# Windowed attention into a two-layer network: even tokens stored first, adjacent heads paired, DMA transposes written straight to their place

## The chip, the cores and the metric

One core of a Trainium2 chip. TensorE (PE) multiplies matrices into PSUM, VectorE (DVE), ScalarE (ACT) and GpSimd (POOL) work on SBUF (DVE and ACT also on PSUM), SyncE (SP) issues most DMAs, and POOL issues those that cast the weights. The metric is the device time of one execution in microseconds (us). Times within the execution come from one profiled run; a line number such as L265 is a line of the kernel before.

## The reference

```python
# q, k, v: 8 batches, 8 heads, 576 tokens, 64 features each
scores = (q @ k.T) / sqrt(64)
scores = where(abs(i - j) <= 32, scores, -1e9)     # a window of 65 tokens
attn = exp(scores - max); attn = attn / sum(attn)
x = (attn @ v), heads side by side                 # 4608 tokens x 512
h = x @ w_in                                       # 512 -> 2048
g = maximum(0.01 * h, h)
out = g @ w_out                                    # 2048 -> 512, float32
```

## The kernel before

**Attention, in tiles.** Heads are taken in pairs, head p with head p + 4, four pairs per batch. A tile is one pair with one half of the tokens (288 of 576): i counts 64 tiles, and `where(i)` gives batch, half and pair. The keys of a pair lie in `kbd` (and the values in `vbd`) in nine blocks of 64 tokens, each block a 128x128 matrix with one head in either diagonal corner and zeros elsewhere, so one matmul serves both heads. Each buffer exists twice, for even and odd batches. A query token sees two neighbouring key blocks, or one near an edge; the table WIN lists per half five (block, first query, count) entries whose columns sum to 544.

For each tile, `score` (L249) runs five matmuls into the PSUM tile `ps`, ACT takes the exponential of 544 columns into `e`, and POOL multiplies by a 0/1 mask (L265) into one of six places of `prob`. The odd blocks' columns lie behind the even blocks' columns, and one of the two parts is 32 columns shorter. `join` (L269) adds the two parts on DVE, reading into zero pads; with it `sums` (L279) needs one matmul with a matrix of ones, without it two (256 and 288 columns). Tiles from JOINED = 12 on are joined. DVE takes the reciprocal (L296). `product` (L299) runs five matmuls with `vbd`, and `scaled` (L320) multiplies by the reciprocal into `xT`, a ring of four halves. PSUM holds one `ps`, one `s` and one `x`.

**Getting queries and keys there.** `load_qk` (L66) puts six consecutive tokens of a head into each of 96 partitions (1536 bytes in a run). `cast_qk` (L177) makes bf16 copies `qb`, `kb`. Transposed, these have the tokens in the order c, i (token 6i + c). For batches 0 to 2 PE transposes them (L214) into PSUM; from batch BY_DMA = 3 on a DMA does, into `tdma` tiles. Either way ACT then copies them to token order (L222 for qT, L228 for kT), and `place_keys` (L235) has DVE copy kT into `kbd`, two copies for a pair.

**The network.** A group g is 288 tokens. `h_tile` (L346) runs four matmuls of 288 columns (L336) for each of 16 feature blocks, and `h_out` (L341) evacuates through ACT with the leaky ReLU into `gT`. `o_tile` (L364) runs 16 matmuls of 512 columns (L373) for 128 tokens; ACT evacuates (L378) and SP stores. Both share four PSUM buffers.

**Order.** Each engine executes its instructions in the order in which the program issues them. The start is written out by hand (L473 to L581): batch 0, the first group and its weight loads (POOL, L465 and L471), then the second half, batch 1 and group 1. From there a plan lists h and o work with a cost each, `due` spreads the four tiles of a group over the time before its start, and `spend` (L608) issues a `step` when one is due. A step issues the join of tile i + 1, transposes, the score of i + 2, then sums, product and scaling of tile i, then key placement, casts, DMA transposes and loads for later batches. The table PLAN and the conditions at L423 to L456 and L630 say in which step of a batch each of those stands.

Of the kernel before, what the change touches and what calls it, by code (L numbers as in the profile page):

```python
# [16 lines left out]
def kernel(  # L17
# [11 lines left out]

    nc = tc.nc  # L30
# [12 lines left out]
    NCOL = 544  # L43
# [10 lines left out]
    tdma = ctx.enter_context(tc.tile_pool(name="tdma", bufs=1))  # L54
# [9 lines left out]

    def load_qk(b, p, behind=None):


        for into, src, name in ((qf, q, "qf"), (kf, k, "kf")):
            t = fload.tile([96, 2, RUN * D], FP32, name=f"{name}{p}")
            if behind is not None:  # L70
                behind.memset(t[0:1, 0, 0:1], 0.0)
                behind = None
            nc.sync.dma_start(  # L73
                out=t, in_=src[b, p:H:NPAIR].rearrange("a (p c) d -> p a (c d)", c=RUN),
            )
            into[b, p] = t

    def load_v(b, p):

        t = fload.tile([128, NB, D], FP32, name=f"vf{p}")  # L80
        for a in range(2):
            nc.sync.dma_start(
                out=t[64 * a:64 * a + 64],
                in_=v[b, NPAIR * a + p].rearrange("(c p) d -> p c d", p=64),
            )
# [30 lines left out]
    def clear(t, p):  # L116
# [12 lines left out]

    PAD = 32  # L130
    SPLIT = [HALF - PAD, HALF]
    WIN = [
        [(1, 32, 128), (3, 160, 128), (0, 0, 96), (2, 96, 128), (4, 224, 64)],
        [(4, 288, 64), (6, 352, 128), (8, 480, 96), (5, 288, 128), (7, 416, 128)],
    ]

    win = const.tile([128, 3, 128], BF16)
    nc.gpsimd.memset(win, 1.0)
    for lo in (0, 64):
# [3 lines left out]
            base=0, channel_multiplier=-1, pattern=[[0, 3], [1, 128]],  # L143
# [3 lines left out]
            base=2 * W, channel_multiplier=1, pattern=[[0, 3], [-1, 128]],  # L147
        )
    nc.gpsimd.memset(vbd[0][:, 3], 0.0)
    win_f = win.rearrange("p n c -> p (n c)")  # L150
    mask = [const.tile([128, NCOL], BF16, name=f"mask{i}") for i in range(2)]

    def make_masks():
        for hf in range(2):
            lo = (0, 2 * W)[hf]
            nc.gpsimd.tensor_copy(
                out=mask[hf][:, 0:SPLIT[hf]], in_=win_f[:, lo:lo + SPLIT[hf]],
            )
            lo = (W, 0)[hf]
            nc.gpsimd.tensor_copy(  # L160
                out=mask[hf][:, SPLIT[hf]:NCOL], in_=win_f[:, lo:lo + NCOL - SPLIT[hf]],
            )
    NPROB = 6
    prob = const.tile([128, NPROB, NCOL + 2 * PAD], BF16)
    nc.vector.memset(prob[:, :, 0:PAD], 0.0)
    nc.vector.memset(prob[:, :, PAD + NCOL:], 0.0)

# [9 lines left out]
    def cast_qk(b, p, q_eng=None):  # L177
        for eng, src, dst in ((q_eng or nc.gpsimd, qf, qb), (nc.gpsimd, kf, kb)):
            tok = src[b, p].rearrange("p a (c d) -> p c a d", d=D)
            if eng is nc.scalar:  # L180
                eng.activation(out=dst[:, p], in_=tok, func=AF.Copy)
            else:
                eng.tensor_copy(out=dst[:, p], in_=tok)  # L183
# [9 lines left out]

    BY_DMA = 3
    qkT, asked = {}, {}

    def transpose_dma(b, p):
        for which, src in (("q", qb), ("k", kb)):
            t = tdma.tile([128, RUN, 96], BF16, name=f"{which}T{p}")
            nc.sync.dma_start_transpose(out=t, in_=src[:, p].rearrange("p c a d -> p (c a d)"))  # L200
            qkT[b, p, which] = t
        asked[b, p] = state["done"]

    def transposes(b):

        qT[b] = attn.tile([128, NPAIR, S], BF16, name="qT")
        for p in range(NPAIR):
            for which, src in (("q", qb), ("k", kb)):
                if b >= BY_DMA:
                    tp = qkT.pop((b, p, which))  # L210
                else:
                    tp = mmps.tile([128, RUN, 96], BF16, name="tp", tag="mm")
                for c in range(RUN if b < BY_DMA else 0):
# [6 lines left out]
                tok = tp.rearrange("p c i -> p i c")  # L220
                if which == "q":
                    nc.scalar.activation(  # L222
                        out=qT[b][:, p].rearrange("p (i c) -> p i c", c=RUN), in_=tok, func=AF.Copy,
                    )
                else:
                    kT = kt.tile([128, S], BF16, name="kT")
                    kT_v = kT.rearrange("p (i c) -> p i c", c=RUN)
                    nc.scalar.activation(out=kT_v, in_=tok, func=AF.Copy)  # L228
# [3 lines left out]
    unplaced = []  # L232

    def place_keys():

        while unplaced:
            b, p, kT = unplaced.pop(0)
            for a in range(2):
                r = slice(64 * a, 64 * a + 64)
                nc.vector.tensor_copy(  # L240
                    out=kbd[b % 2][r, p, :, r],
                    in_=kT[r].rearrange("p (n j) -> p n j", j=64),
# [7 lines left out]
    def score(i):  # L250
        b, hf, p = where(i)
        ps = scps.tile([128, 1024], FP32, name="ps")
        lo = c0 = 512 - SPLIT[hf]
        for blk, q0, n in WIN[hf]:
            nc.tensor.matmul(  # L255
                ps[:, c0:c0 + n], kbd[b % 2][:, p, blk],
                qT[b][:, p, q0:q0 + n], start=True, stop=True,
            )
            c0 += n
        e = attn.tile([128, NCOL], BF16, name="e")  # L260
        nc.scalar.activation(  # L261
            out=e, in_=ps[:, lo:lo + NCOL], func=AF.Exp, scale=scale,
        )
        pr = prob[:, i % NPROB, PAD:PAD + NCOL]
        nc.gpsimd.tensor_mul(pr, e, mask[hf])  # L265
        probs[i] = [pr, None, None]
        state["ps"] = ps

    def join(i):  # L269


        hf = where(i)[1]
        lo = PAD * hf
        t = prob[:, i % NPROB]
        both = joined.tile([128, HALF], BF16, name="both")
        nc.vector.tensor_add(both, t[:, lo:lo + HALF], t[:, lo + HALF:lo + 2 * HALF])  # L276
        probs[i][1] = both

    def sums(i):  # L279
# [6 lines left out]
        else:  # L286
            nc.tensor.matmul(
                s, ones_bd, pr[:, (NCOL - HALF) * (1 - hf):(NCOL - HALF) * (1 - hf) + HALF],
                start=True, stop=False, skip_group_check=True,
            )  # L290
            nc.tensor.matmul(
# [378 lines left out]
```

The softmax here doesn't subtract the row's maximum and nothing guards it: scores larger than these inputs give would overflow.

## Time and profile before

| | us |
|---|---|
| median of 6 runs | 323.42 |
| lowest and highest | 322.3, 323.62 |
| the profiled execution | 323.6 |
| its span | 321.9 |
| PE, ACT, DVE, POOL busy | 304.5, 223.9, 213.9, 182.4 |
| weight loads into PE | 205.5 |
| 40 ACT copies to token order, batches 3 to 7 (L222, L228) | 47.2 |
| 24 ACT evacuations of PE transposes, batches 0 to 2 | 15.7 |
| 144 PE transposes, modelled busy time | 11.6 |
| 64 DVE copies into kbd (L240) | 28.5 |
| 56 POOL casts of q and k (L183) | 48.4 |

The span runs from the first to the last instruction of the profile. Busy times of PE are modelled and overlap one another, so the time that a matmul holds PE is better read from the start of the next one. The clock that was granted to PE was 1.00 in every stretch. In the profile's lines, "idle before <- X" is the time that an engine stood still ahead of such an instruction and what ended it.

### The profile page before, as it was taken

Reading aid. Unit: us, or ns where it says so; the run is one execution under the profiler, and the core shown is the slowest. Engines: PE = TensorE matmul, PEld = TensorE weight load, DVE = VectorE, ACT = ScalarE, POOL = GpSimd, SP = SyncE. Lnnn points to the kernel's source line nnn. Section 1 sums busy time; section 2 is a strip of 40 time slices with the busy share of each in tenths; the row PEclk is TensorE's granted clock in tenths of the full one; section 3 lists DMA queues with packets and bytes.
Section 4 is the critical chain, followed back from the end, with each engine's and each line's share of the span. In section 5 each row is a group of like instructions: output and inputs, shape, how many; then the busy total and the mean of one; then the engine's idle time right before and its main releaser. Section 6 shows DMA issues by size and latency. Waiting matters only on the chain.

```text
span 321.9 us, 6584 instructions
## 1 busy us (share of the span) xinstructions
PE 304.5 (95%) x2497; PEld 205.5 (64%) x2497; DVE 213.9 (66%) x259; ACT 223.9 (70%) x432; POOL 182.4 (57%) x215
## 2 busy tenths in 40 slices
PE   1669999999999999999999999999999999999995
PEld 1457775586765857676664857676665857676653
DVE  5678975976757779677838778677747666565100
ACT  7577594296658897888887887888885837464531
POOL 8799967667946876169623896269612653230000
PEclk9999999999999999999999999999999999999999
DMA  8999999999997999829994399929611000000101
GB/s 178 212 173 225 268 242 217 273 223 227 211 185 197 230 232 234 161 86 173 184 224 124 91 205 221 188 71 138 166 39 65 36 34 35 32 36 0 67 33 66
DMA packets 85168, 48.28 MB, mean 150 GB/s; under 512 B 64016, under 2 KB 80656, under 8 KB 85136
## 3 DMA queue, kind: packets, MB, share of 16 engines
q1 hardware_dynamic: 80848, 43.66, 64.1%
q0 software_dynamic: 4288, 4.20, 8.0%
q8 instruction: 19, 0.31, 0.4%
q14 instruction: 13, 0.11, 0.1%
HBM read 36.70 MB, written 9.44 MB: 143 GB/s over the span
## 4 chain that ended last, share of the span: by engine, by line
PE 84%; DVE 6%; DMA 3%; ACT 2%; POOL 1%; SPq 1%; issue 1%; DVEq 0%; ACTq 0%
PE mm L336 36%; PE mm L373 36%; PE x L307 4%; PE ps L255 4%; DVE r L296 4%; DMA kf<-in_k_dram 3%; PE s L285 2%; DVE xT L322 1%; SPq L73 1%; PE tp L214 1%; DVE qb L183 1%; ACT kT L228 1%; POOL w_in_bf L465 1%; ACT qT L222 1%; DVE kbd L240 1%
## 5 line engine op out<-in xcount | busy, mean ns | idle before, releaser
L296 DVE RECIPROCAL r<-s 128x288 f32<-128x288 f32 x64 | 125.1, 1955 | 56.8 <-PE s L285 53.5
L336 PE MATMUL mm<-xT,w_in_bf 128*128 128x288 bf16 x1024 | 134.0, 286 | 0.3 <-DVE xT L322 0.2
L265 POOL TENSOR_TENSOR prob<-e,mask 128x544 bf16<-128x544 bf16 x64 | 77.8, 1215 | 99.4 <-ACT e L261 81.0
L373 PE MATMUL mm<-w_out_bf,gT 128*128 128x512 bf16 (+2 forms) x592 | 130.4, 373 | 0.0
L342 ACT ACTIVATE gT<-mm 128x288 bf16<-128x288 f32 x256 | 103.6, 414 | 24.2 <-PE mm L336 9.5
L336 PEld LDWEIGHTS <-w_in_bf 128*128 128x128 bf16 x1024 | 97.9, 98 | 24.6 <-issue 0.6
L373 PEld LDWEIGHTS <-gT 128*128 128x128 bf16 x592 | 56.0, 98 | 59.3
L378 ACT ACTIVATE o_sb<-mm 128x512 f32<-128x512 f32 (+2 forms) x37 | 21.7, 586 | 53.2 <-PE mm L373 53.2
L261 ACT ACTIVATE e<-ps 128x544 bf16<-128x544 f32 x64 | 39.8, 621 | 10.5 <-PE ps L255 8.4
L191 POOL CAST vbd<-vf 64x576 bf16<-64x576 f32 x58 | 38.5, 664 | 3.2 <-DMA vf<-in_v_dram 1.4
L240 DVE COPY kbd<-kT 64x576 bf16<-64x576 bf16 x64 | 28.5, 445 | 15.6 <-ACT kT L228 14.9
L322 DVE TENSOR_TENSOR xT<-x,r 128x288 bf16<-128x288 f32 x64 | 29.3, 458 | 8.5 <-PE x L307 1.8
L183 POOL CAST kb<-kf 96x768 bf16<-96x768 f32 x32 | 28.6, 897 | 3.8 <-DMA kf<-in_k_dram 3.7
L255 PEld LDWEIGHTS <-kbd 128*128 128x128 bf16 x320 | 21.5, 99 | 10.2 <-DVE kbd L240 1.4
L255 PE MATMUL ps<-qT,kbd 128*128 128x128 bf16 (+2 forms) x320 | 26.3, 214 | 1.8 <-DVE kbd L240 1.2
L307 PE MATMUL x<-prob,vbd 128*128 128x128 bf16 (+2 forms) x320 | 26.0, 213 | 1.1 <-DVE xT L322 1.0
L307 PEld LDWEIGHTS <-vbd 128*128 128x128 bf16 x320 | 21.4, 99 | 3.9 <-DVE xT L322 1.0
L222 ACT ACTIVATE qT<-qT 128x576 bf16<-128x576 bf16 x20 | 23.6, 1182 | 0.0
L228 ACT ACTIVATE kT<-kT 128x576 bf16<-128x576 bf16 x20 | 23.6, 1182 | 0.0
L276 DVE TENSOR_TENSOR both<-prob 128x288 bf16<-128x288 bf16 x52 | 22.8, 438 | 0.6
L183 POOL CAST qb<-qf 96x768 bf16<-96x768 f32 x24 | 19.8, 824 | 0.0
L285 PE MATMUL s<-both,ones_bd 128*128 128x288 bf16 x52 | 14.9, 286 | 0.0
(45 smaller groups left out, 102.3 us busy)
## 6 DMA issues: line engine op xcount, KB each, us to landing
qf<-in_q_dram SPq DMA_DIRECT2D x32, 288.0 KB, 4.5
kf<-in_k_dram SPq DMA_DIRECT2D x32, 288.0 KB, 4.6
vf<-in_v_dram SPq DMA_DIRECT2D x64, 144.0 KB, 5.0
out_dram<-o_sb SPq DMA_DIRECT2D x35, 256.0 KB, 2.8
w_in_bf<-in_moe_w_in_dram POOLq DMA_DIRECT2D x8, 256.0 KB, 7.3
w_out_bf<-in_moe_w_out_dram POOLq DMA_DIRECT2D x4, 512.0 KB, 15.5
qT<-qb SPq DMA_TRANSPOSE x20, 4.0
kT<-kb SPq DMA_TRANSPOSE x20, 3.3
```

Source lines behind the costliest of these rows:

```text
L183: eng.tensor_copy(out=dst[:, p], in_=tok)
L191: nc.gpsimd.tensor_copy(out=vbd[b % 2][r, p, :, r], in_=vf[b, p][r])
L240: nc.vector.tensor_copy(out=kbd[b % 2][r, p, :, r], in_=kT[r].rearrange("p (n j) -> p n j", j=64),)
L255: nc.tensor.matmul(ps[:, c0:c0 + n], kbd[b % 2][:, p, blk], qT[b][:, p, q0:q0 + n], start=True, stop=True,)
L261: nc.scalar.activation(out=e, in_=ps[:, lo:lo + NCOL], func=AF.Exp, scale=scale,)
L265: nc.gpsimd.tensor_mul(pr, e, mask[hf])
L296: nc.vector.reciprocal(r, s)
L307: nc.tensor.matmul(x[:, a:a + n], vbd[b % 2][:, p, blk, :], pr[:, c0:c0 + n], start=(n_ == 0), stop=(n_ == len(WIN[hf]) - 1), skip_group_c ...
L322: nc.vector.tensor_mul(place(i), x, r)
L336: nc.tensor.matmul(h[:, 0:HALF], w_in_bf[:, c, ts(f, 128)], xT[:, c, ds(g * HALF % RING, HALF)], start=(c == 0), stop=(c == DMC - 1),)
L342: nc.scalar.activation(out=gT[:, f, ds(g * HALF % RING, HALF)], in_=h[:, 0:HALF], func=AF.Prelu, alpha=0.01,)
L373: nc.tensor.matmul(o[:, lo:hi], gT[:, f, ds(128 * j % RING, 128)], w_out_bf[:, f, lo:hi], start=(f == 0), stop=(f == FFC - 1),)
```

## The change

- A pair is heads 2p and 2p + 1. The feature order of x is then the reference's, and a w_in load is one DMA over 128 partitions instead of two over 64.
- From `qT` to the first layer, the 288 tokens of a half are kept with the even tokens first, then the odd ones. Scores, masks, prob, sums, x and xT are in this order; `h_out` puts the tokens back in their order when it reads PSUM. Keys and values keep token order in kbd and vbd: `place_keys` now writes every second element.
- From batch 2 on (BY_DMA = 2), `load_qk` puts tokens in pairs (runs of 512 bytes), each cast is made in two parts, and the transposing DMA writes `qT` and `kT` itself. ACT's copies to token order disappear for these batches. A key pair is placed from two steps after its DMA was asked for.
- Both parts of a tile are 288 columns, the shorter with 32 columns that the mask sets to zero; the exponential and the mask product cover 576. `ps` is one tile that is kept for the whole run.
- JOINED is 9. Casts, transposes and loads of a batch have fixed steps (qk_due, v_due) in place of PLAN. In the start, batch 1's loads stand behind another weight load, and the second half of batch 0 stands at f = 7, 11, 14.

```diff
-    NCOL = 544
+    EVEN = HALF // 2
...
+            heads = src[b, 2 * p:2 * p + 2]
+            if b < BY_DMA:
+                nc.sync.dma_start(out=t, in_=heads.rearrange("a (p c) d -> p a (c d)", c=RUN))
+            else:
+                nc.sync.dma_start(
+                    out=t.rearrange("p a (g e) -> p a g e", g=3),
+                    in_=heads.rearrange("a (g p c) d -> p a g (c d)", g=3, c=2),
+                )
...
     WIN = [
-        [(1, 32, 128), (3, 160, 128), (0, 0, 96), (2, 96, 128), (4, 224, 64)],
-        [(4, 288, 64), (6, 352, 128), (8, 480, 96), (5, 288, 128), (7, 416, 128)],
+        [((0, 0, 48), (2, 48, 64), (4, 112, 32)), ((1, 16, 64), (3, 80, 64))],
+        [((4, 0, 32), (6, 32, 64), (8, 96, 48)), ((5, 0, 64), (7, 64, 64))],
     ]
...
+                by_c = src[b, p].rearrange("p a (g c d) -> c p g a d", g=3, c=2)
+                parts = [(dst[:, p, 3 * c:3 * c + 3], by_c[c]) for c in range(2)]
...
-    BY_DMA = 3
     def transpose_dma(b, p):
-        for which, src in (("q", qb), ("k", kb)):
-            t = tdma.tile([128, RUN, 96], BF16, name=f"{which}T{p}")
-            nc.sync.dma_start_transpose(out=t, in_=src[:, p].rearrange("p c a d -> p (c a d)"))
-            qkT[b, p, which] = t
-        asked[b, p] = state["done"]
+        if b not in qT:
+            qT[b] = attn.tile([128, NPAIR, S], BF16, name="qT")
+        kT = kt.tile([128, S], BF16, name="kT")
+        for t, src in ((qT[b][:, p], qb), (kT, kb)):
+            nc.sync.dma_start_transpose(
+                out=t.rearrange("p (c i) -> p c i", c=RUN),
+                in_=src[:, p].rearrange("p c a d -> p (c a d)"),
+            )
+        landing.append((state["done"], b, p, kT))
...
     def place_keys():
+        while landing and landing[0][0] + 2 <= state["done"]:
+            unplaced.append(landing.pop(0)[1:])
...
-                    out=kbd[b % 2][r, p, :, r],
-                    in_=kT[r].rearrange("p (n j) -> p n j", j=64),
+                    out=kbd[b % 2][r, p, :, r].rearrange("p n (m c) -> p n c m", c=2),
+                    in_=kT[r].rearrange("p (c n m) -> p n c m", c=2, n=NB),
...
+        by_c = qT[b][:, p].rearrange("p (c i) -> p c i", c=2)
+        for n_, blocks in enumerate(WIN[hf]):
+            for blk, i0, n in blocks:
+                nc.tensor.matmul(
+                    ps_v[:, n_, :, i0:i0 + n], kbd[b % 2][:, p, blk],
+                    by_c[:, :, hf * EVEN + i0:hf * EVEN + i0 + n], start=True, stop=True,
+                )
+        e = attn.tile([128, 2 * HALF], BF16, name="e")
+        nc.scalar.activation(out=e, in_=ps[:, P0:P0 + 2 * HALF], func=AF.Exp, scale=scale)
...
     def h_out(g, f, h):
         nc.scalar.activation(
-            out=gT[:, f, ds(g * HALF % RING, HALF)], in_=h[:, 0:HALF], func=AF.Prelu, alpha=0.01,
+            out=gT[:, f, ds(g * HALF % RING, HALF)].rearrange("p (i c) -> p i c", c=2),
+            in_=h[:, 0:HALF].rearrange("p (c i) -> p i c", c=2), func=AF.Prelu, alpha=0.01,
         )
...
-    JOINED = 12
+    JOINED = 9
...
+    for b in range(2, B):
+        for p in range(NPAIR):
+            qk_due.setdefault(8 * (b - 1) + p + (3 if b == 2 else 2), []).append((b, p))
+            v_due.setdefault(8 * (b - 1) + p + 6, []).append((b, p))
...
         place_keys()
+        for b, p in qk_due.get(i, ()):
+            cast_qk(b, p)
+            transpose_dma(b, p)
+            if b + 1 < B:
+                load_qk(b + 1, p)
+        for b, p in v_due.get(i, ()):
+            cast_v(b, p)
+            if b + 1 < B:
+                load_v(b + 1, p)
...
     def load_w_in(f0, f1):
-        for a in range(2):
-            nc.gpsimd.dma_start(
-                out=w_in_bf[64 * a:64 * a + 64, :, f0:f1], in_=w_in_r[a, :, :, f0:f1],
-            )
+        nc.gpsimd.dma_start(out=w_in_bf[:, :, f0:f1], in_=w_in_r[:, :, f0:f1])
...
+    next(h0)
+    next(h0)
+    score(5)
+    load_w_out(1)
     for p in range(NPAIR):
         load_qk(1, p, nc.gpsimd if p == 0 else None)
...
-        if f in (7, 10, 13):
+        if f in (7, 11, 14):
             second_half()
```

## The prediction

> **What bounds the kernel now.** I read the page's totals and slices first, then the table by stretches of 10 us, the groups by shape, the chain of work that ended last, and the timelines of single engines around each gap.
>
> ```profile
> PE 304.5 (95%) x2497; PEld 205.5 (64%) x2497; DVE 213.9 (66%) x259; ACT 223.9 (70%) x432; POOL 182.4 (57%) x215
> ...
> PE   1669999999999999999999999999999999999995
> ...
> PE 84%; DVE 6%; DMA 3%; ACT 2%; POOL 1%; SPq 1%; issue 1%; DVEq 0%; ACTq 0%
> ```
>
> TensorE (PE) is full in every slice from about 25 us to the end. The 70% of ScalarE (ACT) is an average beside it, so an ACT instruction that disappears is worth nothing unless PE waited for it. By stretch:
>
> ```profile
> 40.00:50.00 10.00, 9.57 (x107) 6.95 (x105) 7.72 (x9) 7.98 (x19) 6.12 (x7) 1.00 1.19 235
> 110.00:120.00 10.00, 10.00 (x76) 6.21 (x74) 6.61 (x11) 9.53 (x16) 8.34 (x11) 1.00 1.25 216
> 120.00:130.00 10.00, 9.52 (x84) 6.99 (x82) 8.90 (x11) 8.06 (x18) 5.95 (x7) 1.00 1.23 236
> ```
>
> The columns are the length, then busy time and count of PE, weight loads, DVE, ACT and POOL, then the clock (1.00 throughout), DMA share and GB/s. After 60 us, 120 to 130 is the only whole stretch before the last in which PE is under 10.00; ACT is at 9.53 just before it. Its cause is in PE's timeline:
>
> ```profile
> 121.49 0.28 PE L285 MATMUL s<-both,ones_bd 128*128 128x288 bf16 x1
> 122.05 0.41 PE L307 MATMUL x<-prob,vbd 128*128 128x128 bf16 x5 [0.28 <-DVE xT L322]
> ...
> 126.45 0.41 PE L307 MATMUL x<-prob,vbd 128*128 128x128 bf16 x5 [0.19 <-DVE xT L322]
> ```
>
> In starts, not modelled ends: undisturbed, the s matmul begins 0.24 us after the score and x 0.12 us after s. Here s begins 0.11 us late (121.14 to 121.49) and the two x 0.44 and 0.36 us late: 0.91 us lost. DVE's two copies into kbd stood behind ACT's reordering copies. So two parts can pay: fewer PE instructions, and a shorter start.
>
> **Rows that price the change.**
>
> ```profile
> L342 ACT ACTIVATE gT<-mm 128x288 bf16<-128x288 f32 x256 | 103.6, 414 | 24.2 <-PE mm L336 9.5
> ...
> L322 DVE TENSOR_TENSOR xT<-x,r 128x288 bf16<-128x288 f32 x64 | 29.3, 458 | 8.5 <-PE x L307 1.8 <-PE mm L336 0.5
> ...
> L240 DVE COPY kbd<-kT 64x576 bf16<-64x576 bf16 x64 | 28.5, 445 | 15.6 <-ACT kT L228 14.9
> ...
> L222 ACT ACTIVATE qT<-qT 128x576 bf16<-128x576 bf16 x20 | 23.6, 1182 | 0.0
> ...
> L222 ACT ACTIVATE qT<-tp 128x576 bf16<-128x576 bf16 x12 | 7.8, 648 | 4.8 <-PE tp L214 4.8
> ```
>
> The two L222 rows do the same reordering. Read with a stride from SBUF it takes 1182 ns; from PSUM, 648.
>
> ```profile
> 15.35 0.82 POOL kb L183
> 16.17 2.58 POOL w_in_bf L465 x4
> 18.75 1.25 POOL prob L265
> ...
> 41.91 0.44 DVE kbd L240
> 42.37 0.45 DVE kbd L240
> 42.85 3.00 DVE qb L183
> 45.89 0.68 PE tp L214 x12
> ...
> 68.37 0.26 PE tp L214 x6
> ```
>
> The chain: POOL's weight-load issues hold up a product early on; two kbd copies and a cast hold up transposes at 45.89; a group of six transposes takes 0.26 us of PE.
>
> **1. Transposes of batch 2 leave PE.** 8 groups x 0.26 = **-2.1 us**, all on the bound engine. The DMAs that replace them run on SP's queue. Joining from tile 9 instead of 12 removes three second sum matmuls; the non-joined L291 holds PE 0.11 us (start 56.01 to the next at 56.12), so -0.3. Nine others grow from 256 to 288 columns, by L287's 0.12 against 0.11: +0.1. **Sum -2.3.** Scores and products keep five matmuls and 544 columns per tile, now in two runs each. No matmul here has two runs; contiguous rows are nearest, so no cost.
>
> **2. ACT copies go.** 40 copies x 1.182 = 47.3 us, and 8 evacuations x about 0.65 = 5.2 us, leave ACT. PE waited for these only in the 0.91 us above: **-0.9**. Next late there would be DVE's queue (part 4).
>
> **3. h_out reads its PSUM bank at a stride.** 256 instructions, now even token, odd token, even token, 576 bytes apart. From 512 elements in 597 ns (L378) and 288 in 414, ACT takes 179 ns plus 0.817 per element; that gives 650 for the 576 strided elements of the PSUM row, which took 648. So a stride in PSUM costs nothing there, and I take 414. The other end, from the SBUF row: (1182-179)/576 = 1.74 ns per element, hence 680 ns. PE is the cover: four L336 matmuls take 0.49 us (0.98 per 8 in the chain). At 680 it is gone. [...]
> The exp over 576 instead of 544 columns costs 26 ns more, 64 times, beside PE.
>
> **4. kbd copies write every second element.** 64 DVE copies. The lower end is today's 445. L322 takes 458 ns for 288 elements, and DVE's memsets of 64 and 2304 words (112 and 1978 ns) give 0.83 ns for each further element: 458 + 288 x 0.83 = 698. The upper end is the strided ACT row, 1182. I take 0.70 us, the nearest: same engine. [...]
> In the steady state a step has 4.05 us of dense PE work plus 0.6 of attention, some 4.5 us. DVE needs join 0.44 + reciprocal 1.96 + xT 0.46 + two copies 1.4 = 4.3 in half of the steps, 2.9 in the others: it fits, barely. The copies stand behind xT and two steps ahead of the score that reads them (one in batch 2). No charge.
>
> **5. DMA and POOL in batches 2 to 7.** POOL's product grows from 1215 to about 1286 ns; each q or k cast becomes two. From 664 ns at 576 elements and 824 at 768, 384 take about 0.5. A step's POOL work is 1.3 + 4 x 0.5 = 3.3 us of 4.5, and the product stands first. After the step's product SP issues two transposes (1.2 to 1.3 us each) and lands the last 3.3 us later: about 2.5 + 2.0 + 2.6 + 3.3 = 10.4 us from the step's start. DVE reaches the copy after 9 + 2.9 = 11.9 us: 1.5 us to spare. Loads of q and k have three times the packets, at 512 bytes: between today's 4.5 us and twice the 5.0 of a v load with as many packets; 4.5 is nearer, same bytes. They are asked seven steps ahead (three in batch 2). SP's queue carries the same stores behind them. No charge, bounds 0 to +1.5.
>
> **6. The start.** w_in loads go from two issues each to one of w_out's shape (0.8 us): the 2.58 us before the product of tile 2 becomes 1.6, -1.0. But two kbd copies for pair 3, ending at 19.3, end 0.5 later, at 19.8, and hold the next reciprocal (20.47, or 19.5 without them): what stays is some **-0.6**. At 41.91 two copies cost 0.5 more and the cast behind them starts later; PE already waits 0.4 for it: **+0.5**. Loads of batch 1 start about 1 us later, behind one w_out load, and three joins of 0.3 to 0.5 enter DVE's queue ahead of reciprocals of tiles 8 to 10, where PE waited 0.15 us already: between 0 and +1, taken **+0.3**. Spreading the second half over f = 7, 11, 14 moves waits of 0.24 and 0.34 for the reciprocals without shortening DVE's line: 0.
>
> **Sum.** -2.3 - 0.9 - 0.6 + 0.5 + 0.3 = -3.0 us. The profiled execution took 323.6 us: a span of 321.9 and 1.7 around it. That gives **320.6**. The median of the runs is 323.42, 0.2 under the profiled one. The case's own range is 319.6 to 322.3.
>
> **The rivals.**
> *The start takes it back* (0.15): if the casts wait for batch 1's loads (POOL waited 1.8 us for kf at 42.61, DMA share 1.19), the second pairs and step 8 slip another 1.5 to 2 us: about 322.6.
> *The start gives more* (0.09): kbd copies at 445 ns keep the full -1.0 and drop +0.5: 319.7, with fewer waits 319.2.
> *DVE becomes the bound* (0.08), on the slower side: it decides where a copy exceeds (4.5 - 2.86) / 2 = 0.82 us. At 1182 ns a placing step needs 5.2 us, 0.7 too long; four in a row make 2.8, of which some 1.2 is spare, so 1.6 for each of six batches, and 1.5 more at the start: 332. For it: DVE is already at 8.90 in the stretch above. Against it: DVE's own rows are all under the limit.
> *h_out slow* (0.05): at 680 ns, 16 tiles and two exps need 12.2 us where PE needs 9.0; the four PSUM buffers hide about 2: +1.2 in 15 groups, 339.
> *The DMA path does not serve in time* (0.03): landing 3 us later than reckoned, DVE stops 1.5 us at a copy; a third of it reaching PE in 24 steps gives +12: 333. For it: DMA share above 1 up to 130 us; against it: loads asked seven steps ahead.
>
> **How the numbers follow.** The forecast has 0.60. The range, 318.8 to 323.6, holds the first three cases and leaves out 0.16. About 0.3%, 1 us, is what a measurement of this kernel can tell from no change. Faster: 0.58 of the forecast, 0.09, and 0.03 of the start's rival, 0.70. Same: 0.02 and 0.12, 0.14. Slower: 0.16.
>
> **What would show it.** PE matmuls 2446, no transposes after 51 us, PE 10.00 in each stretch from 60 to 310; no qT<-qT or kT<-kT rows and ACT near 173 us busy; gT<-mm at 414 ns; kbd copies near 700 ns; w_in issues near 0.8. Wrong if gT<-mm is above 0.5 us, if PE waits for kbd or r after 60 us, if POOL waits for qf or kf, or if the first transposes of batch 1's pair 2 come after 46.5 us.

## The result, and the profile after

The changed kernel takes **324.06 us** (median of 19 runs, 323.16 to 325.21). The kernel before took 323.01 in 43 runs beside them (322.3 to 323.67). The ratio is 1.0034, with an interval of 1.0025 to 1.0043: about 1 us slower, where 3 us faster was forecast. The profiled execution of the changed kernel took 323.77 us, a span of 322.1 and 1.7 around it, against 323.6 and 321.9 before. So the two profiled executions differ by 0.2 us, the medians by 1.05. The traces are read for where time was won and lost; that difference of 0.85 is spread between runs, and one execution of each can't place it. One run of experiment 7, of 326.05 us, counts as one in the chip's slower state and is left out of its median there.

The page of the kernel after, its totals, PE's slices and its chain of waits:

```profile
PE 303.3 (94%) x2446; PEld 203.4 (63%) x2446; DVE 226.8 (70%) x263; ACT 179.0 (56%) x384; POOL 198.1 (62%) x259
...
PE   2679899999989999999999999999999999999996
...
PE 81%; DVE 10%; POOL 3%; issue 2%; ACT 1%; DMA 1%; DVEq 0%; POOLq 0%; ACTq 0%
```

PE has the 2446 matmuls that were forecast, 51 fewer. ACT fell from 223.9 to 179.0 us. DVE rose by 13 us, and its share of the chain from 6% to 10%: more of the chain runs through DVE now. The table by stretches of the kernel after, with the columns of the same table before:

```profile
40.00:50.00 10.00, 8.94 (x97) 6.65 (x95) 7.10 (x8) 8.24 (x20) 5.25 (x7) 1.00 1.21 249
...
80.00:90.00 10.00, 9.29 (x70) 6.01 (x68) 5.94 (x8) 5.90 (x14) 5.58 (x7) 1.00 1.17 179
90.00:100.00 10.00, 9.17 (x68) 5.67 (x69) 6.58 (x9) 3.95 (x8) 4.78 (x7) 1.00 1.01 213
120.00:130.00 10.00, 10.00 (x86) 7.29 (x85) 8.52 (x11) 6.27 (x15) 7.21 (x9) 1.00 0.83 182
```

The stall at 121 to 126 us is gone (10.00 where 9.52 stood). In its place 40 to 50 lost more (8.94 after 9.57), and a new hole stands on both sides of 90 us. The groups by shape of the kernel after that the forecast had priced:

```profile
L350 ACT ACTIVATE gT<-mm 128x288 bf16<-128x288 f32 x256 | 103.8, 413 | 23.7 <-PE mm L343 5.2
...
L255 DVE COPY kbd<-kT 64x576 bf16<-64x576 bf16 x64 | 47.8, 747 | 8.6 <-ACT kT L238 4.5 <-DMA kT<-kb 3.5
...
L438 POOL DMA_DIRECT2D w_in_bf<-in_moe_w_in_dram x4 | 3.3, 820 | 0.0
```

All three stand near their forecast: 413 ns (414), 747 ns (700), 820 ns (0.8 us). No single mean is far off, and yet the sum is.

**Where the time went.** PE runs the same attention tiles in the same order in every version, so the start of a tile's first score matmul in PE's timeline is a common mark. In us from the span's start; the rows other than the first two are told below:

```
score of tile           4      9     14     18     19     28     63
before              21.44  47.28  64.18  84.37  89.38 130.62 287.36
after               22.00  48.63  65.81  84.13  90.83 131.15 287.89
after - before      +0.56  +1.35  +1.63  -0.24  +1.45  +0.53  +0.53
unit step           21.13  46.83  64.61  82.80  89.16 129.48 286.22
token order         21.01  46.45  64.30  82.75  89.76 130.08 286.82
step 2 in before    21.54  48.82  65.73  86.63  91.86 133.35 290.09
mended              20.79  46.25  63.28  81.41  86.42 126.73 283.47
mended - before     -0.65  -1.03  -0.90  -2.96  -2.96 -3.89  -3.89
```

The kernel after loses 1.6 us up to tile 14, wins 1.9 where the transposes of batch 2 left PE, loses 1.7 in front of tile 19, and wins 0.9 at 121 to 126 us. So both promised gains are there, and two losses of 1.6 and 1.7 us stand against them.

**The first loss: copies that wait beside POOL.** Rows of the kbd copies, with the shortest, median and longest duration in ns. The kernel before:

```profile
L240 DVE COPY kbd<-kT x64: 399/448/451, 7.7 to 244.9; 64x576 bf16<-64x576 bf16 x64
```

The kernel after:

```profile
L255 DVE COPY kbd<-kT x64: 495/678/2954, 7.8 to 266.4; 64x576 bf16<-64x576 bf16 x64
```

Before, 64 copies are all alike. After, one of them takes six times another. What sets it is in the timelines of DVE and then of POOL, kernel after (start, length, then the instruction; in brackets the idle time before it):

```profile
42.62 1.05 DVE L255 COPY kbd<-kT 64x576 bf16<-64x576 bf16 x2 [1.97 <-ACT kT L238]
43.69 0.56 DVE L196 CAST qb<-qf 96x768 bf16<-96x768 f32 x1
45.09 3.48 DVE L255 COPY kbd<-kT 64x576 bf16<-64x576 bf16 x2 [0.84 <-ACT kT L238]
```

```profile
45.25 0.97 POOL L196 CAST kb<-kf 96x768 bf16<-96x768 f32 x1 [2.89 <-DMA kf<-in_k_dram]
46.16 2.04 POOL L549 MEMSET vbd<- 128x1152 bf16 x2
```

With POOL idle the pair of copies takes 1.05 us. Beside POOL's cast and memsets the next pair takes 3.48, and the score of tile 9, which reads these keys, starts at 48.63 after PE had waited 1.06. The pair ends at 48.57, 0.37 us after the second memset (48.20). The whole kernel shows the same: 55 of its 64 copies begin while a cast, memset or product of POOL is running, and each of the 55 ends 0.36 to 0.40 us after the end of such an instruction. So the copy stands until POOL's instruction is done, here through three of them in a row, and then needs its 0.37 us. In the kernel before, the end of a copy has no such tie to POOL (0.09 to 0.43 us after an end, or none within the copy). A like spread was to be read in the kernel before, in DVE's cast of the queries, which the forecast passed over:

```profile
L183 DVE CAST qb<-qf x7: 714/1318/2986, 4.8 to 46.7; 96x768 bf16<-96x768 f32 x7
```

Seven equal casts, from 714 to 2986 ns. The 3.00 us cast at 42.85, shown in the prediction, ran beside POOL's cast and memsets of the kernel before and ended 0.41 us after them:

```profile
42.61 0.82 POOL L183 CAST kb<-kf 96x768 bf16<-96x768 f32 x1 [1.80 <-DMA kf<-in_k_dram]
43.38 2.05 POOL L578 MEMSET vbd<- 128x1152 bf16 x2
```

The kbd copies around it kept 0.45.

**The second loss: batch 2's keys come late.** SP's queue issues the transposes and the loads. Its timeline in the kernel after:

```profile
78.59 1.46 SPq L211 DMA_TRANSPOSE qT<-qb  x1
80.16 1.20 SPq L211 DMA_TRANSPOSE kT<-kb  x1
81.42 0.57 SPq L81 DMA_DIRECT2D qf<-in_q_dram  x1
82.04 0.50 SPq L81 DMA_DIRECT2D kf<-in_k_dram  x1
82.58 1.30 SPq L91 DMA_DIRECT2D vf<-in_v_dram  x2
83.98 1.83 SPq L211 DMA_TRANSPOSE qT<-qb  x1
85.92 1.93 SPq L211 DMA_TRANSPOSE kT<-kb  x1
```

The queue has hardly a gap. POOL's cast of pair 3's keys ended at 79.10 (the line "77.70 1.40 POOL L196 CAST kb<-kf" of its timeline), but their transpose was issued from 85.92 to 87.85. Then DVE, and then PE, in the kernel after:

```profile
86.77 0.46 DVE L329 TENSOR_TENSOR xT<-x,r 128x288 bf16<-128x288 f32 x1
89.74 1.03 DVE L255 COPY kbd<-kT 64x576 bf16<-64x576 bf16 x2 [2.52 <-DMA kT<-kb]
```

```profile
84.74 4.57 PE L343 MATMUL mm<-xT,w_in_bf 128*128 128x288 bf16 x36
90.83 0.41 PE L270 MATMUL ps<-qT,kbd 128*128 128x96 bf16 x5 [1.51 <-DVE kbd L255]
```

DVE stood 2.52 us for the transfer, whose issue had begun 3.8 us earlier, and PE 1.51 us for DVE.

### The profile page after: what moved, and what is told of

Read it like the earlier page. It is cut to its first block, busy times and chain, and to the rows that moved or that the text cites. A ratio compares the mean times of both kernels' runs of the same rounds, so it can differ in the third digit from the quotient of the medians.

```text
span 322.1 us, 6482 instructions
## 1 busy us (share of the span) xinstructions
PE 303.3 (94%) x2446; PEld 203.4 (63%) x2446; DVE 226.8 (70%) x263; ACT 179.0 (56%) x384; POOL 198.1 (62%) x259
## 4 chain that ended last, share of the span: by engine, by line
PE 81%; DVE 10%; POOL 3%; issue 2%; ACT 1%; DMA 1%; DVEq 0%; POOLq 0%; ACTq 0%
PE mm L343 35%; PE mm L382 35%; DVE r L304 5%; PE x L315 4%; PE ps L270 4%; DVE kbd L255 4%; PE s L296 2%; DVE xT L329 1%; DMA kT<-kb 1%; POOL kb L196 1%; POOL prob L277 0%; ACT e L275 0%; PE tp L224 0%; ACT vbd L202 0%; POOL win L147 0%
## 5 line engine op out<-in xcount | busy, mean ns | idle before, releaser
L277 POOL TENSOR_TENSOR prob<-e,mask 128x576 bf16<-128x576 bf16 x64 | 81.7, 1276 | 84.8 <-issue 42.4
L255 DVE COPY kbd<-kT 64x576 bf16<-64x576 bf16 x64 | 47.8, 747 | 8.6 <-ACT kT L238 4.5
L275 ACT ACTIVATE e<-ps 128x576 bf16<-128x576 f32 x64 | 41.4, 647 | 17.7 <-PE ps L270 16.1
L204 POOL CAST vbd<-vf 64x576 bf16<-64x576 f32 x58 | 40.3, 695 | 1.7
L196 POOL CAST kb<-kf 96x384 bf16<-96x384 f32 (+1 forms) x56 | 36.0, 663 | 4.8 <-DMA kf<-in_k_dram 4.7
L270 PEld LDWEIGHTS <-kbd 128*128 128x128 bf16 x320 | 20.5, 99 | 15.4 <-DVE kbd L255 6.6
L196 POOL CAST qb<-qf 96x384 bf16<-96x384 f32 x48 | 24.4, 535 | 0.0
L287 DVE TENSOR_TENSOR both<-prob 128x288 bf16<-128x288 bf16 x55 | 20.8, 378 | 0.8
L224 PE MATMUL tp<-ident,qb 96*128 96x96 bf16 x48 | 4.4, 242 | 5.8 <-DVE qb L196 5.7
L224 PEld LDWEIGHTS <-qb 96*128 96x128 bf16 x48 | 3.5, 117 | 6.8 <-DVE qb L196 6.4
```

What stands on the lines that cost most here:

```text
L196: eng.tensor_copy(out=to, in_=tok)
L204: nc.gpsimd.tensor_copy(out=vbd[b % 2][r, p, :, r], in_=vf[b, p][r])
L255: nc.vector.tensor_copy(out=kbd[b % 2][r, p, :, r].rearrange("p n (m c) -> p n c m", c=2), in_=kT[r].rearrange("p (c n m) -> p n c m", c=2 ...
L270: nc.tensor.matmul(ps_v[:, n_, :, i0:i0 + n], kbd[b % 2][:, p, blk], by_c[:, :, hf * EVEN + i0:hf * EVEN + i0 + n], start=True, stop=True,)
L275: nc.scalar.activation(out=e, in_=ps[:, P0:P0 + 2 * HALF], func=AF.Exp, scale=scale)
L277: nc.gpsimd.tensor_mul(pr.rearrange("p n c i -> p (n c i)"), e, mask[hf].rearrange("p n c i -> p (n c i)"),)
```

## The experiments

The theory after the first reading was that the form of the kbd copy (every second element) made it wait for POOL, and that the lateness of batch 2 was a matter of SP's queue or of full DMA engines. Rivals were that the 512-byte packets of the new loads were the cause, and that the earlier joins or the order of the start's loads were. Where the quoted expectations use letters for theories, the text names them in words. Times are medians; a ratio is against the kernel before, run beside it, which had medians of 322.96 to 323.1, and need not be the quotient of two medians. A wait of PE is the bracket in its timeline, the idle time ahead of the instruction named.

### 1. The copy at unit step

```diff
-                    out=kbd[b % 2][r, p, :, r].rearrange("p n (m c) -> p n c m", c=2),
+                    out=kbd[b % 2][r, p, :, r].rearrange("p n (c m) -> p n c m", c=2),
```

> The changed kernel with the keys written to kbd in runs of 32 with step 1 (even tokens of a block first) instead of every second element; all 64 copies keep their size and count. The mask and the values do not follow this order, so the keys are weighted wrongly: only the time counts. [...] Rival B (the copies are longer because POOL has more work in the changed kernel, whatever their step): they stay near 750 ns and the time stays at 324.

322.28 us, ratio 0.9987 (0.9967 to 1.0006), 1.8 less than the kernel after. The row of the copies:

```profile
L255 DVE COPY kbd<-kT x64: 302/499/952, 7.8 to 264.5; 64x576 bf16<-64x576 bf16 x64
```

That the time fell fits the theory, and not the rival's 324; the reason holds in part only: without the step the copy is shorter still than before (0.30), but it varies threefold. So it isn't the step that makes a copy wait: 51 copies begin beside POOL here too, and all end 0.17 to 0.21 us after an instruction of POOL, where it was 0.36 to 0.40. None stood through three of POOL's instructions in a row, as one did there. PE still waits 1.19 us ahead of the score of tile 19, at 89.16, which the copy's form does not touch.

### 2. Token order in batches 0 and 1, so that their copies keep the form of before

```diff
-                        out=kT.rearrange("p (c i e) -> p c i e", c=2, e=RUN // 2),
-                        in_=tok, func=AF.Copy,
+                        out=kT.rearrange("p (i c) -> p i c", c=RUN),
+                        in_=tp.rearrange("p c i -> p i c"), func=AF.Copy,
...
+                if b < BY_DMA:
+                    nc.vector.tensor_copy(
+                        out=kbd[b % 2][r, p, :, r],
+                        in_=kT[r].rearrange("p (n j) -> p n j", j=64),
+                    )
+                    continue
```

> The changed kernel, but for batches 0 and 1, which PE transposes, ACT writes kT in token order as before, and the 16 copies into kbd are step 1 again; the other 48 are unchanged. Theory A: the loss of the start (0.7 us at 38 us, 1.36 us at 47 us against the kernel before) is the price of these copies next to POOL; the score at 48.6 moves to about 47, and the time falls by 1.3 to 1.8 us to about 322.5. Rival C (the start lost its time to batch 1's loads, which stand behind one more weight load, and to three more joins): the time falls by 0.4 us at most.

322.79 us, 0.9995 (0.9981 to 1.001): 1.3 less than after. The rows of its two kinds of copies:

```profile
L261 DVE COPY kbd<-kT x48: 498/664/823, 71.3 to 265.3; 64x576 bf16<-64x576 bf16 x48
L256 DVE COPY kbd<-kT x16: 385/447/450, 7.8 to 50.7; 64x576 bf16<-64x576 bf16 x16
```

The 16 copies of the start are back at 447, and the score of tile 9 starts 2.2 us earlier than in the kernel after. At tile 19 only 1.1 of them are left. Of the other 1.1, 0.67 us go between tiles 9 and 14, which take 17.85 us for 17.18; experiments 7 and 8 come back to that. The rest goes at batch 2's keys: PE waits 1.82 us for the last of them where it waited 1.51. PE comes to that wait 1.38 us earlier than in the kernel after (87.94 for 89.32) and leaves it 1.07 earlier (89.76 for 90.83), so what is won ahead of it is partly waited away there.

### 3. The other direction: the new copy in the kernel before

All 64 copies (first diff), then those of batches 0 and 1 alone (second):

```diff
-                    out=kbd[b % 2][r, p, :, r],
-                    in_=kT[r].rearrange("p (n j) -> p n j", j=64),
+                    out=kbd[b % 2][r, p, :, r].rearrange("p n (m c) -> p n c m", c=2),
+                    in_=kT[r].rearrange("p (c n m) -> p n c m", c=2, n=NB),
```

```diff
+                if b < 2:
+                    nc.vector.tensor_copy(
+                        out=kbd[b % 2][r, p, :, r].rearrange("p n (m c) -> p n c m", c=2),
+                        in_=kT[r].rearrange("p (c n m) -> p n c m", c=2, n=NB),
+                    )
+                    continue
```

> The kernel before with one part of the change alone: the 64 copies into kbd write every second element and read runs of 32, as in the changed kernel. kT stays in token order, so the keys end up in another order than the mask and the values: only the time counts. Theory A: the copies take 445 ns or a little more where POOL is idle and up to 1.7 us or more beside it, the first halves of batches 0 and 1 lose 1 to 1.5 us as in the changed kernel, and the time rises to about 324.4. Rival B: copies at 445 ns, 323.1.

> The kernel before with the step-2 copies into kbd in batches 0 and 1 alone (16 of 64); the keys of these two batches end up in another order than the mask and the values, so only the time counts. All 64 copies gave 2.8 us. In their profile PE had lost 1.4 us by the score at 48 us and another 0.7 at 75. Theory A: 16 copies beside POOL's start give 1.3 to 2.0, 324.6 or so; the other 48 the rest. If the steady state's copies give most, 323.5.

All 64: 325.79 us, 1.0084 (1.0067 to 1.0101), +2.8. The 16 alone: 325.06, 1.0062 (1.0045 to 1.0079), +2.1. The copy's form costs by itself nearly as much as the forecast promised in all, and most of it in batches 0 and 1. DVE and then PE of the first of the two:

```profile
45.91 2.85 DVE L240 COPY kbd<-kT 64x576 bf16<-64x576 bf16 x2
```

```profile
48.82 0.41 PE L255 MATMUL ps<-qT,kbd 128*128 128x128 bf16 x5 [1.22 <-DVE kbd L240]
```

Sorting each kernel's copies by whether a cast, memset or product of POOL lay over more than half of them, or over under a twentieth, gives one table (ns, median, and the longest beside POOL):

```
copy                             alone    beside POOL   longest
before (run of 576 into 9 x 64)  445      445            451
unit step, runs of 32            321      523            952
step 2, in before                514      829           2336
step 2, after                    514      714           2954
```

The copy of before takes 445 ns whatever POOL did. In the lower three rows a copy beside POOL takes 0.2 to 0.3 us more in the median, and 2.4 more at worst. Shown is that the form decides, and that a copy of the new form lasts until POOL's instruction beside it has ended; why the form decides is not shown. No run here moved POOL's work away.

### 4. Loads of values earlier, or on another queue

```diff
-            if 10 <= i < 14:
-                load_v(2, i - 10)
+            if 8 <= i < 12:
+                load_v(2, i - 8)
```

> The changed kernel with the loads of batch 2's values two steps earlier (tiles 8 to 11 instead of 10 to 13). Theory D (SP's queue: transposes 2.6, q and k loads 1.1, v loads 1.3 and a store 0.6 us make 5.6 us of issue time for each of steps 11 to 14, which last 4.5, so the fourth pair's transposes are issued 5 us after their casts): they now issue within 2 us of the casts, the wait of 2.5 us of DVE for kT and of 1.67 us of PE at 89 us go, and the time falls by about 1.8 us to 322.2. Rival E (the 16 DMA engines are the limit there, at a share of 1.1 to 1.2): the same bytes only move earlier, into a stretch as full, and half of the wait or more stays.

324.92 us, 1.0061 (1.0044 to 1.0079), worse than after. The wait moved from pair 3 to pairs 0 and 1 (PE 0.26 us ahead of 75.68, 1.86 ahead of 82.26). The issues of the loads at 60 us, in SP's queue:

```profile
60.61 1.31 SPq L81 DMA_DIRECT2D qf<-in_q_dram  x1
61.97 1.10 SPq L81 DMA_DIRECT2D kf<-in_k_dram  x1
63.16 1.93 SPq L91 DMA_DIRECT2D vf<-in_v_dram  x2
```

One load of queries costs SP 1.31 us here and 0.57 at 81.42 above. An issue is not a fixed cost. The trace shows only its length, not what made it longer. The second try gave these loads to ACT's queue:

```diff
-    def load_v(b, p):
+    def load_v(b, p, q=nc.sync):
...
-            nc.sync.dma_start(
+            q.dma_start(
...
-                load_v(2, i - 10)
+                load_v(2, i - 10, nc.scalar)
```

> The changed kernel with the same eight loads of batch 2's values at the same steps, issued from ACT's queue instead of SP's. The bytes and their time are unchanged, only SP's issue time is relieved of 1.3 us in each of four steps. Theory D: the wait at 89 us goes and the time falls by about 1.8 us to 322.2. Rival E (DMA engines full): the wait stays, 324.

330.0 us, 1.0217 (1.0186 to 1.0248). The wait for batch 2's keys did go, but at the price of worse ones. The waits of this kernel in 50 to 110 us (total, times, longest):

```profile
PE mm L343 <- ACT gT L350: 4.8, 2, 3.2
ACT gT L350 <- DMA kf<-in_k_dram: 4.1, 1, 4.1
ACT gT L350 <- DMA out_dram<-o_sb: 3.8, 1, 3.8
```

Two of ACT's pairs of issues took 4.49 and 4.41 us where others took 1.39; behind each ACT stood, 4.1 and 3.8 us, until by the profile another transfer had ended, and PE stood for ACT. So it is not on SP alone that issues differ in length; on what the length hangs is not shown. Whether relieving SP would have been enough this run can't tell: PE came to tile 18 at 90.94 us, 6.8 later than in the kernel after, so the keys had that much more time.

### 5. Batch 3's loads out of the way

The kernel after asks for batch 3's queries and keys right behind each transpose of batch 2. Here they come later:

```diff
-            if b + 1 < B:
+            if b + 1 < B and b > 2:
                 load_qk(b + 1, p)
...
+        if 14 <= i < 18:
+            load_qk(3, i - 14)
```

> The changed kernel with the loads of batch 3's queries and keys three steps later (tiles 14 to 17 instead of 11 to 14; their casts stand at 18 to 21). This takes 2.3 MB out of the stretch in which batch 2's transposes run, from SP's queue and from the DMA engines alike, and nothing of batch 2 moves. Theory E, as the two runs before left it (between 55 and 90 us the DMA engines have more to move than they can, so every transfer of that stretch is late, whichever queue it is issued from and in whichever order): the wait for kT and the 1.7 to 1.9 us of PE around 89 us go, 324.1 becomes 322.3. Rival F (batch 2's transposes are simply asked for one step too late for their landing of 3 to 4 us): the wait stays above 1 us, 323.5 or more.

324.0 us, 1.0026 (1.0003 to 1.005). Its twelve runs fall in two groups, 322.2 to 322.9 and 324.0 to 325.9. Two rows of its table by stretches:

```profile
20.00:30.00 10.00, 8.63 (x78) 6.78 (x78) 7.81 (x8) 6.91 (x15) 6.76 (x9) 0.83 1.15 182
...
80.00:90.00 10.00, 10.00 (x84) 6.97 (x83) 8.66 (x11) 6.16 (x14) 6.77 (x9) 1.00 0.93 184
```

The hole at 90 us is gone, as expected, and the DMA share there fell from 1.17 to 0.93. The median didn't follow. The first row shows a granted clock of 0.83 far from the edit. But this execution took 322.93 us and belongs to the lower group, as does the other of the twelve with a lower mean clock (0.995, 322.39 us), so the dip is not what makes the higher group. Experiment 7 has a candidate for it.

### 6. Rival: the 512-byte packets

All batches load in runs of 1536 bytes again:

```diff
-            if b < BY_DMA:
+            if True:
                 nc.sync.dma_start(out=t, in_=heads.rearrange("a (p c) d -> p a (c d)", c=RUN))
```

> The changed kernel with q and k of batches 2 to 7 loaded in runs of 1536 bytes as before (192 packets instead of 576). Their tokens then stand in an order that nothing else follows, so the attention of these batches is over wrong tokens: only the time counts. Theory E with the packets as its cause: three times the packets cost the full stretch, and the wait at 89 us goes, 322.4. Rival G (the 512-byte packets took 35 ns each against 95 for 1536 bytes, so only 10% more engine time; what filled the stretch are the eight transposes of batch 2, some 670 packets each): the wait shrinks by 0.5 us at most, 323.6 or more.

324.44 us, 1.0045 (1.0027 to 1.0062), with PE's wait still there, 1.42 us ahead of 91.58. Packet times summed over 52 to 96 us and divided by 16 engines, for 44 us of time: 46.0 before, 49.2 after, 46.3 here. So this kernel moves no more DMA time than the one before, and waits as the one after: it is not the amount. The two mended kernels below confirm it with 47.1 and 50.5 in the same stretch and no wait at tile 19. What differs is how soon SP comes to pair 3's keys: 6.8 us after their cast in the kernel after, 6.7 here, 3.2 and 3.1 there. Before, the same crowded queue held nothing that was needed soon, since PE transposed batch 2 itself. (By the packet counts of the two kernels a transpose has 608 packets, not some 670.)

### 7. Both mends, and the order of the start

Token order (2) with deferred loads (5); token order with batch 1's loads back ahead of the load of w_out, as before the change (diff below); all three:

```diff
-    next(h0)
-    next(h0)
-    score(5)
-    load_w_out(1)
...
+    next(h0)
+    next(h0)
+    score(5)
+    load_w_out(1)
```

> The changed kernel with both: kT of batches 0 and 1 in token order, so that their copies are step 1, and the loads of batch 3's queries and keys three steps later. If the two losses are what kept the change from its gain, they add: 324.1 - 1.3 - 1.8 = 321.0, 0.6% under the kernel before. If the second is only shifted into the first's place (the earlier start makes the transfers later still), 322.

> The changed kernel with kT of batches 0 and 1 in token order and with batch 1's loads ahead of the second w_out load again, as in the kernel before. Against the run with the token order alone (322.8): if the later loads cost the second pairs of batch 1 their time (POOL waited 2.9 us for kf at 45.3, 1.8 us before), 0.3 to 0.8 us less, 322.2; if the copies were all of it, no change within 0.3.

> The changed kernel with three of its parts mended: step-1 copies for batches 0 and 1, batch 3's queries and keys loaded three steps later, batch 1's loads ahead of the second w_out load. If the three gains are separate (1.3, then about 1.9, then 0.9 us), 320.0, 1.0% under the kernel before. If the third only brought the same wait forward, 320.9 as without it.

Token order and deferral: 320.46 us (seven runs, 319.88 to 322.85), 0.9939 (0.9915 to 0.9963). Token order and old order of the loads: 321.91, 0.9972 (0.9957 to 0.9987), 0.9 less than token order alone, though the two intervals overlap. All three: 320.72, 0.9944 (0.9918 to 0.9969), no less than the first. The medians of the first and third don't price the order, since both kernels again have a higher group of runs (up to 322.85 and 323.05). The marks place its gain: tiles 9 to 14 take 17.85 us with token order alone and 17.02 with the old order of the loads as well (46.63 to 63.65), against 16.90 before. The first has a new wait, in its PE timeline and ahead of it in DVE's:

```profile
120.71 0.28 PE L302 MATMUL s<-both,ones_bd 128*128 128x288 bf16 x1 [1.26 <-DVE r L310]
```

```profile
116.24 1.93 DVE L261 COPY kbd<-kT 64x576 bf16<-64x576 bf16 x2 [2.65 <-DMA kT<-kb]
```

Batch 3's loads, put off by three steps, now made batch 3 late. This profiled execution took 322.85 us and is of the higher group; from tile 19 to tile 28 it needs 42.96 us. The profiled executions of experiment 5 and of all three mends, with the same three steps but in their lower groups, need 40.31. So this wait comes in some executions and not in others, and its 2.65 us are about the distance between the groups. That it makes the higher group of experiment 5 too is likely but not shown, since no high run of it was profiled. So the last one puts them off by two:

```diff
-        if 14 <= i < 18:
-            load_qk(3, i - 14)
+        if 13 <= i < 17:
+            load_qk(3, i - 13)
```

> The same with batch 3's loads two steps later instead of three. Theory E, with an account of DMA engine time (between 52 and 96 us some 50 us of packets against 44): the loads may move only so far that batch 3's casts, at tile 18, still find them; with three steps a profile showed POOL and then PE late at 119 us. Two steps should then show neither wait, 320.0 with fewer high runs; if the stretch is still too full, PE waits at 88 us again, 321.5.

**319.59 us** (four runs, 319.31 to 319.9), 0.9898 (0.9883 to 0.9914), in the table of marks as "mended". Its page, SP's queue, and PE at the place of the old hole:

```profile
PE 301.2 (95%) x2426; PEld 203.6 (64%) x2446; DVE 222.8 (70%) x263; ACT 178.7 (56%) x384; POOL 197.5 (62%) x259
...
PE 88%; DVE 5%; POOL 3%; issue 1%; ACT 1%; DVEq 0%; POOLq 0%; ACTq 0%
```

```profile
78.07 1.59 SPq L211 DMA_TRANSPOSE qT<-qb  x1
79.77 2.29 SPq L211 DMA_TRANSPOSE kT<-kb  x1
82.12 0.57 SPq L81 DMA_DIRECT2D qf<-in_q_dram  x1
```

```profile
86.42 0.40 PE L276 MATMUL ps<-qT,kbd 128*128 128x96 bf16 x5
```

Pair 3's keys are issued at 79.77 instead of 85.92. The transpose takes longer to issue (2.29 us), yet nothing waits: the score of tile 19 has no bracket. DVE's share of the chain is 5%. (The page counts 2426 matmuls beside 2446 weight loads: 20 matmul records are missing from this trace.)

### 8. Rival: the joins from tile 9

```diff
-    JOINED = 9
+    JOINED = 12
```

> The changed kernel with step-1 copies for batches 0 and 1 and with JOINED back at 12. Against the run with the step-1 copies alone (322.8): three joins leave DVE between 54 and 63 us, where PE waits 1.0 us in three places for xT, and three second sum matmuls (0.37 us) come back. My part 6 priced the joins' delay with the later loads at +0.3: then no change within 0.3. If the waits for xT are the joins' alone, 0.6 less: 322.2.

> The mended kernel (step-1 copies for batches 0 and 1, batch 1's loads earlier, batch 3's loads two steps later: 319.6) with JOINED back at 12. With the wait at 82 to 88 us in the profile, JOINED = 12 gave 0.8 us, which could be its own or that wait's. If the three early joins cost 0.3 as part 6 had it, less the 0.3 of the second matmuls: 319.6. If the joins cost what that run showed: 318.8.

With token order alone: 321.96 us, 0.997 (0.9956 to 0.9984), 0.8 less. On the mended kernel: **319.40**, 0.9894 (0.9874 to 0.9913), 0.2 less and inside the interval. By the marks the 0.8 lies ahead of batch 2: tiles 9 to 14 take 16.94 us here (46.22 to 63.16) where token order alone takes 17.85, while tiles 14 to 19 take 0.3 longer than there. On the mended kernel, with batch 1's loads early, the same stretch takes 17.03 with joins from tile 9 and 16.94 with joins from 12. So the early joins and the late loads together cost 0.9, and undoing either one wins back 0.8 to 0.9; the joins alone cost 0.1. This is the fastest version, 3.6 us under before and 4.7 under after.

## Why the prediction was wrong

**Part 1 held.** The intervals from one PE start to the next, without those that hold a recorded wait, sum to 296.8 us after and 298.9 before: -2.1, forecast -2.3. The two-run matmuls cost nothing: a score or product of 128 columns holds PE 56 ns (median) in both kernels. **Part 2 held**: the 0.91 us is gone. **Part 3 held**: gT<-mm at 413 ns, where 414 was forecast.

**Part 4 failed, in "No charge".** The mean price was right (747 ns for 700), as was the size of the steady state: after tile 19 the kernel after runs beside before without losing. What failed was to price the copy as a fixed duration. It is 0.51 us alone and up to 2.95 beside POOL, and at the start, where POOL fills buffers and casts, it stood directly ahead of a score. The range for one copy ended at 1182 ns; the longest took 2954. A row that bore on it was in the profile of before, the cast of 714 to 2986 ns, which the prediction showed in its chain and read as a fixed 3.00.

**Part 6 failed in its sum**, +0.2 forecast for the start and +1.6 measured at tile 14. The -0.6 from w_in came out as forecast once the copies were harmless (-0.65 at tile 4 in the mended kernel), but as +0.56 in the kernel after: score 2 stood behind the copies of pair 2 (15.20 to 16.88), POOL's mask product of tile 2 waited 1.09 us for its exponential, and score 3 waited 0.67 for the copies of pair 3, which ended at 20.74 and not at 19.8. The +0.5 at 41.91 was +0.79 from tile 4 to tile 9, by one pair at 3.48 us. The +0.3 for the order of the loads and the joins was right in the kernel after (+0.28 from tile 9 to tile 14), but it grew to 0.9 once the copies of the start were mended.

**Part 5 failed in "1.5 us to spare"**, and in "SP's queue carries the same stores behind them. No charge": it counted a transpose as issued after its cast. For pair 3 of batch 2 SP came to the keys 6.8 us after the cast had ended (79.10 to 85.92), because the queue was filled with pair 2's transposes and loads for batches 2 and 3. In batches 3 to 7 the estimate held: SP came to the keys 0.0 to 2.2 us after their cast, and DVE waited for no kT.

**The rivals.** "The start takes it back" had the place right; its mechanism, casts waiting for loads, is at most part of the +0.28 behind tile 9; the larger share was the copy. With the late loads kept and the copies alone mended (experiment 2), nothing is lost up to there (46.45 for 47.28 before). "The DMA path does not serve in time" had the effect of the second loss, "DVE stops 1.5 us at a copy" (2.52 measured), but by a late landing, where the issue was late, and in 24 steps, where it was one place: 1.7 us rather than 12. By the marks either loss alone would have left some 1.1 us of the 2.8 won; the two together turned the sign. The forecast had them as alternatives, and the result, 324.06, lies 0.5 above the range.

**The forecast's gain exists.** With those two obstacles and the order mended, the same idea gives 319.59, 3.4 us under before, where 3.0 was forecast. By the marks of the two profiled executions, which differ by more (3.9), it is -0.9 at the start, -2.1 in batch 2, -0.9 at 121 to 126.

Open: how the 0.85 us by which medians and profiled executions disagree comes about, and whether the late batch 3 of experiment 7 is what parts the two groups of runs in experiment 5.

## What to carry to other kernels

When an edit changes the form of an access, look at the spread of a row and not only at its mean: a row whose longest is several times its shortest, as 714 to 2986 ns here, may be waiting for another engine, and the price to take is the one beside that engine's work at the place where it is needed. When work moves to a queue, follow the queue's own timeline at the first place where it is used, with all that is asked of it there; the steady state may be free while the first round is not (here SP came to the keys at most 2.2 us after their cast in batches 3 to 7, and 6.8 us for the last pair of batch 2). A gain ahead of a wait for a transfer was not a gain here until the wait was mended, so a single mend can be worth less, and sometimes more, than its price: of the 324.06 us, token order alone took 1.3, the deferred loads alone 0.1, both together 3.6.

## What the runs showed of the hardware

- The dependence of the DVE copy into kbd on POOL changed with its form alone: 0.40 to 0.45 us whatever POOL does (before), against 0.30 to 0.95 (unit step, experiment 1) or 0.50 to 2.95 us (every second element, the kernel after). In the latter two forms a copy that begins beside POOL ends 0.17 to 0.21 (experiment 1) or 0.36 to 0.40 us (the kernel after) behind an instruction of POOL.
- A DMA issue of the same kind did not always hold its engine for the same time: a load of queries held SP 1.31 us in experiment 3 and 0.57 in the kernel after, two loads of values held ACT 4.49 us at one place of experiment 4 and 1.39 at others.
- Packets of 512 bytes took 35 ns each (mean of the kernel after), those of 1536 bytes 95 (mean of the kernel before): a tenth more per byte.
- The granted clock early on was not the same in the profiled executions. Its record begins, at full, at 16.1 us in before, 18.0 in after and 18.5 in experiment 1. Ahead of it PE was slower (six transposes 0.67 us at 13.1 us of before, 0.42 at 16.2), so the prediction's "1.00 throughout" does not cover the first 16 us. This is not the first loss: of these three the record of experiment 1 begins latest, and it has no loss at tile 4 (21.13). In experiment 5 the clock was back at half from 20.8 to 24.3 us.
